# Top-k attention and an exact-GELU MLP: the order of searches, reciprocals and larger halves on DVE, and two more items in 36 by squares

## The chip, the cores and the metric

The kernel runs on one NeuronCore of a Trainium2 chip. The metric is the device time of one execution in microseconds. The core's engines run their own instruction streams and wait for each other by semaphores: TensorE (PE), VectorE (DVE), ScalarE (ACT), GpSimd (POOL), and SyncE (SP), which here issues nearly all DMAs.

## The reference

Attention over 8 batches, 8 heads, 576 rows, head size 64, that keeps the 32 largest scores of each row, and behind it an MLP of 4608 tokens, 512 to 2048 to 512, with exact GELU; all in float32:

```python
scores = scale * np.matmul(q, k.transpose(0, 1, 3, 2))
kth = np.partition(scores, -top_k, axis=-1)[..., -top_k:-top_k + 1]
scores = np.where(scores >= kth, scores, -1e9)
attn = np.exp(scores - max); attn = attn / (sum(attn) + 1e-09)
x = (attn @ v) -> (tokens, heads * 64)
out = gelu(x @ w_in) @ w_out
```

## The kernel before

**Items.** An item is 128 query rows of a pair of heads: a tile of 128 partitions by 2 x 576 scores. There are 18 items for each batch, N = 144 in all. A ring is 36 items (`RINGS = 36`), two batches; places in it repeat, so "item 5 of 36" stands for items 5, 41, 77 and 113.

**Slots.** The whole program is written out by a Python loop over n (L1205), one slot for each item, and the order in which it emits instructions is the order of each engine's stream. Slot n works on several items at once:

- PE makes the scores of items n + 2 (and n + 3); ACT copies them out of PSUM (`scores`, L396).
- DVE makes the larger of each score and its partner 288 columns on (`larger`, L442, row L446). POOL makes the smaller ones from an integer sum (`sum_up` L472, `smaller` L481). The first two searches then need only half the columns. Items 18 to 27 of the first ring (`SINGLE`) go without and are searched over all 576.
- DVE finds the 32 largest of item n in four rounds (`top_k`, L487): MAX8 gives eight largest, MATCH_REPLACE8 strikes them out, for each of the two heads. The first round writes the tile `first`, whose first value is the row maximum. The second pair of rounds searches all 576.
- `threshold` (L522): two small POOL instructions make the bias terms from the 32nd largest value and the maximum (L527, L528).
- `select` and `softmax` (L542, L552): ACT pushes what is below the threshold far down (Prelu, L547), and makes the exponentials with their sum (L559). These are for item n - 1 in slot n. `add_small` (L536, row L540, POOL) adds 1e-9 to the sum, `inverse` (L530, row L534, DVE) takes the reciprocal, `normalise` (L566, row L582, POOL) multiplies.
- Item n - 2 is turned over, so that keys lie on partitions. In one way PE transposes it (one transposition of the ends, L666, eight of the rest, L680) and ACT copies the result out of PSUM into the tile `pt` (L669, L695). In the other way, "by squares", DVE transposes squares of 32 x 32 in place (`square_p`, L610, row L614, in the middle of `top_k(n)`), SP writes the tile to DRAM in four DMAs (`write_p`, L616, row L624) and reads it back one slot later in another order (`read_p`, L626, row L634) into `pt`. From item 27 on, even items go by squares (but for 12 of 36), and of the odd ones those in `LATER` (L594), in the rings after the first and up to item 135 (`moved`, L596).
- The product with v (`attend`, L729, row L751) is made for a pair of items, even and odd, which share the single `pt` tile, in slot n of odd item n - 3, right behind the scores. Where the odd item is one of `LATER`, it is made one slot later, between pieces of the MLP.
- Between all this PE works off pieces of the MLP in a fixed number for each slot (`room_in`, L1141; `bare`, L1137, gives two pieces to a slot whose product has moved away and takes them from the slot before): first layer (L820), gelu on ACT (L836), second layer (L976, L938, L941, and `seven`, L974, which ACT copies out by L995).

**What sets the order around the change.** DVE's stream at the end of slot n, by `last()` (L1346): last search of item n, larger halves of n + 2 where `few[0]` holds (slots from 13 on), reciprocal of n - 1. Then come, in slot n + 1, the squares of new q and k tiles (L294 to L298), where there are any, and the first search of n + 1. On POOL stand in slot n, in this order, `smaller(n + 1)`, `add_small(n - 1)`, `threshold(n)`, `normalise(n - 1)`, `sum_up(n + 2)`, then sums of the MLP. `lists` (halves) and `first` have two buffers each, `pt` has one, the score tiles `s` seven.

Of the kernel before, what the change touches and what calls it, by code (L numbers as in the profile page):

```python
# [14 lines left out]
def kernel(  # L15
# [19 lines left out]
    nc = tc.nc  # L35
    f32, i32, u32 = mybir.dt.float32, mybir.dt.int32, mybir.dt.uint32
# [5 lines left out]
    P = 128  # L42
# [20 lines left out]
    work = ctx.enter_context(tc.tile_pool(name="work", bufs=2))  # L63
# [46 lines left out]
    def flush():  # L110
        held[0] = False
        while late_issues:
            late_issues.pop(0)()
        late_issues.extend(later)
        later.clear()
# [142 lines left out]
    for b in range(B):  # L258
# [4 lines left out]
        last = [(b * NP + p, NM) for p in range(0, NP, 2)]  # L263
# [8 lines left out]
    N = len(items)  # L272
# [4 lines left out]
    few = [False]  # L277
# [55 lines left out]
    S_of, stat_of = {}, {}  # L333
# [95 lines left out]
    lists_of = {}  # L429
    HS = S // 2  # L430

    def paired(i):

        return PAIRED <= i < N and i not in SINGLE

    def halves_of(i):
        s = S_of[i].rearrange("p (e h n) -> p e h n", e=2, h=2)
        return s[:, :, 0], s[:, :, 1]
# [3 lines left out]
    def larger(i):  # L442

        if paired(i) and i not in have_larger:
            have_larger.add(i)
            nc.vector.tensor_tensor(lists_for(i)[:, :, 0], *halves_of(i), op=ALU.max)  # L446

    def into_of(i):

        if i < 2 and i not in into_lists:  # L450
            into_lists[i] = work.tile([P, 2, 2, HS], f32, tag="pt", bufs=1, name="into")
        return into_lists.get(i, lists_of[i])
# [13 lines left out]
    def lists_for(i):  # L466

        if i not in lists_of:
            lists_of[i] = work.tile([P, 2, 2, HS], f32, tag="lists", name="lists")
        return lists_of[i]  # L470
# [10 lines left out]
    def smaller(i):  # L481

        if paired(i):
            both, top = lists_of[i][:, :, 1].bitcast(i32), lists_of[i][:, :, 0].bitcast(i32)
            nc.gpsimd.tensor_tensor(into_of(i)[:, :, 1].bitcast(i32), both, top, op=ALU.subtract)  # L485

    def top_k(i, last, middle):  # L487


        stat_of[i] = st = {  # L490
            "first": work.tile([P, 2, 8], f32, tag="first", name="first"),
        }
        stat = work.tile([P, 4, 2], f32, tag="stat", name="stat")
        st.update((n, stat[:, x]) for x, n in enumerate(("neg", "bias", "den", "rden")))
        top = work.tile([P, 2, 16], f32, tag="top", bufs=1, name="top")
        into = [st["first"]] + [
            top[:, :, 8:16] if r == TOPK // 8 - 1 else top[:, :, 0:8] for r in range(1, TOPK // 8)
        ]
        if paired(i):
            t = lists_of[i]  # L500
            u = into_of(i)
            both = u.rearrange("p e h n -> p e (h n)")
            rounds = [(t[:, :, 0], u[:, :, 0]), (u[:, :, 0], u[:, :, 0])]
            rounds = [(*(rounds[r] if 16 * r < TOPK else (both, both)), x) for r, x in enumerate(into)]
        else:
            s = S_of[i].rearrange("p (e n) -> p e n", e=2)
            t = work.tile([P, 2, S], f32, tag="lists", name="rest")
            rounds = [(s if r == 0 else t, t, x) for r, x in enumerate(into)]
        for r, (src, dst, x) in enumerate(rounds):
            if 16 * r == TOPK:  # L510
                middle()
            for e in range(2):
                nc.vector.max(x[:, e], src[:, e])  # L513
            if r < len(rounds) - 1:
                for e in range(2):
                    nc.vector.match_replace(dst[:, e], x[:, e], src[:, e], LOWEST)  # L516
            if r == len(rounds) - 1:
                last()

        st["kth"] = top[:, :, 15]  # L520

    def threshold(i):  # L522

        if i < 0 or i >= N:
            return
        st = stat_of[i]
        nc.gpsimd.tensor_scalar(st["neg"], st["kth"], -1.0, None, op0=ALU.mult)  # L527
        nc.gpsimd.tensor_tensor(st["bias"], st["kth"], st["first"][:, :, 0], op=ALU.subtract)  # L528

    def inverse(i):  # L530
        if i < 0 or i >= N:
            return
        st = stat_of[i]
        nc.vector.reciprocal(st["rden"], st["den"])  # L534

    def add_small(i):  # L536
        if i < 0 or i >= N:
            return
        st = stat_of[i]
        nc.gpsimd.tensor_scalar(st["den"], st["den"], 1e-9, None, op0=ALU.add)  # L540
# [50 lines left out]
            return i % RINGS != RINGS // 2 - 1  # L591
        return moved(i) or (i % 2 == 0 and i % RINGS != 12)

    LATER = (3, 13, 25, 31)  # L594

    def moved(i):  # L596

        return RINGS <= i < N - 8 and i % RINGS in LATER

# [7 lines left out]
    RINGS = 2 * len(items) // B  # L607
    turned = {}

    def square_p(i):  # L610

        if squared(i):
            s = S_of[i]
            nc.vector.transpose(s, s)  # L614

    def write_p(i):  # L616

        if squared(i):
            turned[i] = d = dram.tile([SQ, NJ + NM, P // SQ, P], f32, tag="turned", name="turned")
            s = S_of.pop(i).rearrange("p (x j) -> p x j", j=SQ)  # L620
            d = d.rearrange("i c k n -> i (c k) n")
            for a in range(P // SQ):
                rows = slice(a * SQ, (a + 1) * SQ)
                nc.sync.dma_start(out=d[:, :, rows], in_=s[rows])  # L624
# [498 lines left out]
    def mlp(n):  # L1123
        for _ in range(n):
            if done[0] >= len(pieces) or pieces[done[0]][0] > ready[0] or left[0] == 0:
                return
            pieces[done[0]][1]()
            done[0] += 1
            left[0] -= 1
            if eager[0]:  # L1130
                run_gelus()
                run_small(9)
# [58 lines left out]
    first = {2: (0, 1, 1), 3: (2, 2, 3)}  # L1191
    prep_in, squares_in = {}, {}
    for pair in range(2, n_pairs):
        b, p = divmod(pair, NP)
# [10 lines left out]
    for n in range(ahead):  # L1205
# [87 lines left out]
        if few[0]:  # L1293
            room = ODD if n % 2 else 0
            if mid and (mid[0] in starts_next or mid[0] % RINGS == LATER[0]):
                mlp(1)
# [34 lines left out]
            softmax(n - 1, 1)  # L1331
        if n > 0:
            smaller(n + 1)
        add_small(n - 1)
        for piece in tr[-1:] + prep:
            piece(None)
            mlp(1)
# [6 lines left out]
        run_gelus()  # L1344
        if n < N:
            def last():  # L1346
                if few[0]:
                    larger(n + 2)
                inverse(n - 1)

            top_k(n, last, lambda: square_p(n - 2))
            write_p(n - 2)
            flush()
            if n == 0:
                larger(1)
        else:
            inverse(n - 1)
        threshold(n)
        if n == 0:
            smaller(1)  # L1360
        normalise(n - 1)
# [59 lines left out]
```

## Time and profile before

| | |
|---|---|
| median of 3 runs | 1461.84 us (1461.5 to 1461.9) |
| the profiled execution | 1461.3 us |
| its span, first to last instruction | 1459.5 us |
| granted TensorE clock | 1.0 |
| DVE: searches L513 over 576 columns, lists | 528 of 739 ns |
| DVE: larger halves L446 | 133 of 799 ns |
| DVE: squares L614 | 68 of 1365 ns |
| POOL: normalise L582 | 135 of 2109 ns |

The profile gives for each engine the time in which it was busy; a row of the timeline gives start, length, engine, line, operation, tiles (written <- read) and, in brackets, an idle time ahead of it with what ended it. A row with "x8" merges eight instructions of one kind; its length goes from the first's start to the last's end. Matmuls overlap: the time from one start to the next is less than the length of one. A row of grouped instructions ends in busy time, mean length in ns, and the engine's idle time ahead of them. A row of stretches has the stretch, its length, then busy time and count for PE, weight loads, DVE, ACT and POOL.

### The profile page before, as it was taken

The numbers are of one execution on the slowest core, as the hardware profiler recorded it, in microseconds if no ns is written. First come the engines' busy times: TensorE is split into PE (matmuls) and PEld (weight loads), VectorE is DVE, ScalarE is ACT, GpSimd is POOL, SyncE is SP. The second block draws the span as 40 slices with busy tenths as digits, with TensorE's granted clock in tenths as the row PEclk, the third lists the DMA queues.
The fourth block names the chain that finished last, engine by engine and source line by source line (L and its number), as shares of the span: only waits on it lengthen the run. The fifth ranks groups of instructions, "written<-read, shape, count | busy, mean of one in ns | idle before, by whom it ended". The sixth has DMA issues, their size and how long they took to land.

```text
span 1459.5 us, 26550 instructions
## 1 busy us (share of the span) xinstructions
PE 1442.6 (99%) x8621; PEld 1123.9 (77%) x8621; DVE 1329.6 (91%) x3339; ACT 1056.4 (72%) x1883; POOL 1128.4 (77%) x1290
## 2 busy tenths in 40 slices
PE   8999999999999999999999999999999999999999
PEld 6776678877777777787777778787777777787887
DVE  7999999999999999999999999999999999999601
ACT  7999977777777777767777777777676767677620
POOL 6877657877798878878888878887788887878632
PEclk9999999999999999999999999999999999999999
DMA  7524310045454446456554365456554444543200
GB/s 196 150 87 126 84 48 1 9 98 104 90 113 89 87 87 142 82 113 128 111 99 96 65 117 116 90 112 127 117 102 106 90 80 84 127 98 85 53 15 15
DMA packets 591819, 136.49 MB, mean 94 GB/s; under 512 B 504352, under 2 KB 583232, under 8 KB 591680
## 3 DMA queue, kind: packets, MB, share of 16 engines
q1 hardware_dynamic: 590416, 134.37, 43.5%
q8 instruction: 68, 1.11, 0.3%
q14 instruction: 71, 0.58, 0.1%
q10 hardware_dynamic: 1200, 0.39, 0.1%
q0 software_dynamic: 64, 0.03, 0.0%
HBM read 85.19 MB, written 49.55 MB: 92 GB/s over the span
## 4 chain that ended last, share of the span: by engine, by line
PE 44%; POOL 11%; DVE 7%; issue 3%; ACT 3%; DMA 1%; SPq 0%; DVEq 0%; POOLq 0%; ACTq 0%
PE h_ps L820 17%; PE y_ps L976 11%; PE o L751 5%; PE s_ps L408 3%; POOL s L582 3%; DVE top L513 3%; DVE lists L516 2%; POOL lists L485 2%; POOL lists L477 2%; PE seven L974 2%; PE tp L680 2%; PE y_ps L938 2%; PE y_ps L941 1%; DMA turned<-s 1%; DVE s L614 1%
## 5 line engine op out<-in xcount | busy, mean ns | idle before, releaser
L820 PE MATMUL h_ps<-xT,w_in_sb 128*128 128x256 f32 (+1 forms) x2560 | 533.0, 361 | 0.0
L820 PEld LDWEIGHTS h_ps<-xT,w_in_sb 128*128 128x128 f32 x2560 | 438.9, 191 | 69.2 <-issue 10.9
L513 DVE MAX8 top<-lists 128x8 f32<-128x576 f32 (+1 forms) x792 | 475.9, 641 | 0.0
L547 ACT ACTIVATE s<-s,stat 128x576 f32<-128x576 f32 x288 | 219.2, 786 | 123.0 <-POOL stat L527 122.9
L516 DVE MATCH_REPLACE8 lists<-top,lists 128x288 f32<-128x288 f32 (+1 forms) x528 | 308.0, 589 | 0.0
L582 POOL TENSOR_TENSOR s<-s,stat 128x1152 f32<-128x1152 f32 x135 | 284.8, 2109 | 10.1 <-DVE stat L534 5.3
L559 ACT ACTIVATE s<-s,stat 128x576 f32<-128x576 f32 x288 | 225.2, 787 | 7.6
L485 POOL TENSOR_TENSOR lists<-lists 128x576 int32<-128x576 int32 x132 | 186.6, 1413 | 3.1
L477 POOL TENSOR_TENSOR lists<-s 128x576 int32<-128x576 int32 x133 | 188.2, 1415 | 0.0
L540 POOL TENSOR_SCALAR stat<-stat 128x2 f32<-128x2 f32 x144 | 44.4, 309 | 163.0 <-ACT s L559 156.1
L751 PE MATMUL o<-pt,raw_v 128*64 128x256 f32 x1280 | 152.9, 384 | 1.0 <-ACT pt L685 0.4
L416 ACT ACTIVATE s<-s_ps 128x1024 f32<-128x1024 f32 x127 | 126.4, 1046 | 35.2 <-PE s_ps L408 35.0
L751 PEld LDWEIGHTS o<-pt,raw_v 128*64 128x64 f32 x1280 | 86.8, 136 | 80.9 <-issue 38.1
L976 PE MATMUL y_ps<-w_out_sb,sum 128*128 128x256 f32 x472 | 140.4, 379 | 0.0
L408 PE MATMUL s_ps<-kt,qm 64*128 64x512 f32 x512 | 131.2, 621 | 1.1 <-ACT s L414 0.8
L836 ACT ACTIVATE g<-h_ps 128x512 f32<-128x512 f32 x144 | 78.2, 595 | 66.6 <-PE h_ps L820 66.0
L446 DVE TENSOR_TENSOR lists<-s 128x576 f32<-128x576 f32 x133 | 106.2, 799 | 17.8 <-ACT s L381 5.8
L976 PE MATMUL y_ps<-w_out_sb,g 128*128 128x256 f32 x480 | 116.4, 382 | 0.0
L516 DVE MATCH_REPLACE8 lists<-first,lists 128x288 f32<-128x288 f32 x264 | 114.4, 439 | 0.0
L513 DVE MAX8 first<-lists 128x8 f32<-128x288 f32 x268 | 105.8, 434 | 0.0
L976 PEld LDWEIGHTS y_ps<-w_out_sb,g 128*128 128x128 f32 x480 | 90.4, 190 | 15.0 <-issue 3.1
L976 PEld LDWEIGHTS y_ps<-w_out_sb,sum 128*128 128x128 f32 x472 | 89.8, 190 | 12.1
(162 smaller groups left out, 2359.0 us busy)
## 6 DMA issues: line engine op xcount, KB each, us to landing
turned<-s SPq DMA_DIRECT2D x272, 144.0 KB, 3.6
pt<-turned SPq DMA_DIRECT2D x272, 144.0 KB, 3.2
raw_v<-in_v_dram SPq DMA_DIRECT2D x64, 128.0 KB, 2.5
raw_q<-in_q_dram SPq DMA_DIRECT2D x112, 72.0 KB, 2.3
raw_k<-in_k_dram SPq DMA_DIRECT2D x112, 72.0 KB, 2.4
out_dram<-y SPq DMA_DIRECT2D x30, 256.0 KB, 3.1
w_out_sb<-in_moe_w_in_dram SPq DMA_DIRECT2D x14, 511.8 KB, 4.9
w_out_sb<-in_moe_w_out_dram SPq DMA_DIRECT2D x10, 511.8 KB, 4.1
```

The source lines that it names most:

```text
L408: nc.tensor.matmul(s_ps[:, e], lhsT=q_t[rows, :], rhs=kt[rows, main_keys(pair)], start=True, stop=True)
L416: nc.scalar.activation(spread(s, S + TL, SM), s_ps, func=AF.Copy, scale=scale)
L477: nc.gpsimd.tensor_tensor(t[:, :, 1].bitcast(i32), a.bitcast(i32), b.bitcast(i32), op=ALU.add)
L485: nc.gpsimd.tensor_tensor(into_of(i)[:, :, 1].bitcast(i32), both, top, op=ALU.subtract)
L513: nc.vector.max(x[:, e], src[:, e])
L516: nc.vector.match_replace(dst[:, e], x[:, e], src[:, e], LOWEST)
L547: nc.scalar.activation(s, s, func=AF.Prelu, bias=st["neg"][:, e : e + 1], scale=1.0, alpha=STEEP)
L559: nc.scalar.activation(s, s, func=AF.Exp, bias=st["bias"][:, e : e + 1], scale=1.0, accum_out=st["den"][:, e : e + 1],)
L582: nc.gpsimd.tensor_tensor(s, s, wide, op=ALU.mult)
L751: nc.tensor.matmul(o[e * D : (e + 1) * D, 0:n], lhsT=vt[:, j, e, :], rhs=pt[:, e * NJ + j if j < NM else NM, :], start=(j == 0), stop=(j = ...
L820: nc.tensor.matmul(h_tile(u)[:, i, :], lhsT=w_in_sb[:, ko, f * P : (f + 1) * P], rhs=xT[:, ko, c0 : c0 + n], start=(ko == 0), stop=(ko == ...
L976: nc.tensor.matmul(acc[names][:, k], lhsT=lhsT, rhs=rhs, start=(j == 0 and k == 0), stop=(j == FT // 2 - 1 and k == 1),)
```

## The change

- `top_k(i)` no longer makes the first search of its own item always: `first_max(i)` makes it once and remembers it, and `top_k` takes what is there.
- `last()`, behind the last search of item n, now makes the first search of n + 1 ahead of all else (slots 13 on). The larger halves of n + 2 follow there only in slots 15, 17, 19 and 23 of 36 in the rings after the first (`LATE`), and in slot 34 of every ring; in the other slots they are left to the beginning of slot n + 1, where `larger(n + 1)` stood already for what had not been made, and so come behind the reciprocal and ahead of the squares of q and k.
- In the slots of `LATE`, POOL gets `threshold(n)` ahead of `add_small(n - 1)`.
- `LATER` gains 5 and 23: items 41, 77, 113 and 59, 95, 131 go by squares, and their products a slot later.

```diff
-        stat_of[i] = st = {
-            "first": work.tile([P, 2, 8], f32, tag="first", name="first"),
-        }
+        stat_of[i] = st = {"first": first_max(i)}
...
-            for e in range(2):
+            for e in range(2 if r else 0):
                 nc.vector.max(x[:, e], src[:, e])
...
-            if r == len(rounds) - 1:
-                last()
-
         st["kth"] = top[:, :, 15]
+        last()
+
+    first_of = {}
+
+    def first_max(i):
+
+        if i not in first_of:
+            first_of[i] = x = work.tile([P, 2, 8], f32, tag="first", name="first")
+            src = lists_of[i][:, :, 0] if paired(i) else S_of[i].rearrange("p (e n) -> p e n", e=2)
+            for e in range(2):
+                nc.vector.max(x[:, e], src[:, e])
+        return first_of[i]
...
-    LATER = (3, 13, 25, 31)
+    LATE = (15, 17, 19, 23)
+    LATER = (3, 5, 13, 23, 25, 31)
...
-        add_small(n - 1)
+        late_exps = RINGS < n < N - 1 and n % RINGS in LATE
+        if not late_exps:
+            add_small(n - 1)
...
             def last():
-                if few[0]:
+                if few[0] and n + 1 < N:
+                    first_max(n + 1)
+                if late_exps or few[0] and n % RINGS == RINGS - 2:
                     larger(n + 2)
+                if late_exps:
+                    threshold(n)
+                    add_small(n - 1)
                 inverse(n - 1)
...
-        threshold(n)
+        if not late_exps:
+            threshold(n)
```

## The prediction, made before the result was known

> **What bounds the kernel now.** I read the first part of the page, then the busy time by stretches, then the timeline of one ring (the 36 items 72 to 107, from 695.8 to 1037.8 us). Fences of the timeline give rows in order of time, with other engines' rows left out. A slot n is the stretch from DVE's first search of item n to that of item n + 1.
>
> ```profile
> PE 1442.6 (99%) x8621; PEld 1123.9 (77%) x8621; DVE 1329.6 (91%) x3339; ACT 1056.4 (72%) x1883; POOL 1128.4 (77%) x1290
> 695.80:1037.80 342.00, 341.01 (x2014) 266.06 (x2012) 332.98 (x839) 249.08 (x450) 283.51 (x323) 1.00 0.52 105
> 906.12 5.35 PE L820 MATMUL h_ps<-xT,w_in_sb 128*128 128x256 f32 x24
> ```
>
> In the ring PE is busy 341.0 of 342.0 us and DVE 333.0 (the first and third numbers behind the comma in the second row). Busy time of matmuls proves little, since they overlap. What proves it is their spacing: 24 matmuls in 5.35 us, the last one taking 0.38, are 0.216 us from start to start, and the same spacing holds in nearly every group of the ring. So PE streams without a hole. DVE has 9 us of idle time per ring. PE is the bound, DVE is second by 9 us.
>
> The holes that PE does have, in slot 25 (item 97's) and, first, slot 23:
>
> ```profile
> 915.83 1.39 PE L762 MATMUL o<-pt,raw_v 128*64 128x64 f32 x40 [0.26 <-ACT p L995]
> ...
> 932.93 0.76 DVE L446 TENSOR_TENSOR lists<-s 128x576 f32<-128x576 f32 x1
> 933.02 0.75 POOL L540 TENSOR_SCALAR stat<-stat 128x2 f32<-128x2 f32 x1
> 933.85 0.22 POOL L527 TENSOR_SCALAR stat<-top 128x2 f32<-128x2 f32 x1
> 934.10 1.44 ACT L547 ACTIVATE s<-s,stat 128x576 f32<-128x576 f32 x2 [3.62 <-POOL stat L527]
> 937.35 0.59 PE L976 MATMUL y_ps<-w_out_sb,sum 128*128 128x256 f32 x2
> 937.83 0.38 ACT L995 COPY p<-seven 128x256 f32<-128x256 f32 x1
> 938.26 0.49 PE L373 MATMUL tp_t<-kt,qm 128*128 128x128 f32 x2 [0.32 <-ACT p L995]
> ```
>
> This is the chain that ties PE to DVE in odd slots: last search of the item (DVE), threshold (POOL L527), selection (ACT L547, two halves), gelu (L836, not shown), copy of `seven` (L995), which frees the PSUM bank for the keys matmul (PE L373). Two matmuls of L976 take 0.43 us of PE, so L373 was due at 937.78 and came 0.48 late. The room that the same chain has in slot 11, two slots behind the place where item 5 will now be multiplied:
>
> ```profile
> 802.79 0.38 ACT L995 COPY p<-seven 128x256 f32<-128x256 f32 x1
> 803.43 0.39 PE L373 MATMUL tp_t<-kt,qm 128*128 128x128 f32 x2
> ```
>
> From 803.17 to 803.43: 0.26 us. The two engines run in step, with little between them.
>
> **Part one: items 5 and 23 by squares** (41, 77, 113, 59, 95, 131: six items; 131 is still below 136). PE loses the transposes of L666 and L680 and keeps the keys matmul.
>
> ```profile
> 785.82 1.04 PE L680 MATMUL tp<-ident,s 128*128 128x128 f32 x8
> 786.70 0.60 PE L976 MATMUL y_ps<-w_sum,g 128*128 128x256 f32 x2
> 787.13 0.59 PE L976 MATMUL y_ps<-w_out_sb,sum 128*128 128x256 f32 x2
> 787.66 1.99 PE L408 MATMUL s_ps<-kt,qm 64*128 64x512 f32 x8
> ```
>
> From start to start the eight take 0.88 us, 0.11 each; with the one of L666 it is 0.99 per item, 5.9 for six. Against it: the item's product with v (L751, 20 matmuls) leaves its place behind the scores and goes a slot later between two MLP pieces, as item 97's does now:
>
> ```profile
> 971.00 0.60 PE L941 MATMUL y_ps<-w_out_sb,g 128*128 128x256 f32 x2
> 971.53 2.38 PE L751 MATMUL o<-pt,raw_v 128*64 128x256 f32 x20
> 973.84 0.70 PE L938 MATMUL y_ps<-w_out_sb,g 128*128 128x256 f32 x2
> 974.37 0.60 PE L941 MATMUL y_ps<-w_out_sb,g 128*128 128x256 f32 x2
> ```
>
> A pair of pieces takes 0.43; here 0.53 before the group and 0.53 behind it. Behind scores these two tenths are paid by the scores anyway (787.13 to 787.66 is 0.53 too). So 0.2 us per item comes back, 1.2 for six. PE saves 4.7 net. ACT loses the copies out of PSUM (L669, L695) and gains nothing; the number of MLP pieces is unchanged, two go from slots 7 and 25 to 8 and 26.
>
> DVE gains one transpose per item:
>
> ```profile
> L614 DVE STREAM_TRANSPOSE s<-s x68: 1355/1366/1373, 298.7 to 1362.5; 128x1152 f32<-128x1152 f32 x68
> turned<-s SPq DMA_DIRECT2D x272, 144.0 KB, 3.6
> ```
>
> 1.37 us each, 2.7 per ring: 333.0 + 2.7 = 335.7, against PE's 342.0 - 1.6 = 340.4. DVE stays second by over 4 us, so I cost it at nothing in the sum. If the cover were gone it would cost 8.2. SP gets four writes and four reads more per item, 48 over the run. A write lands after 3.6, a read likewise, and from the square in slot i + 2 to the product in slot i + 4 there are more than one and a half slots, some 15 us (342.0 / 36 = 9.5 a slot). What stands behind them in that queue are loads of q, k and v, which are early. I take nothing.
>
> **Part two: the order on DVE.** Now, behind an item's last search, come larger halves of n + 2 (L446), reciprocal of n - 1 (L534), and only then the next item's first search.
>
> ```profile
> 749.73 1.40 DVE L513 MAX8 top<-lists 128x8 f32<-128x576 f32 x2
> 751.24 0.78 DVE L446 TENSOR_TENSOR lists<-s 128x576 f32<-128x576 f32 x1
> 751.39 0.67 POOL L528 TENSOR_TENSOR stat<-top,first 128x2 f32<-128x2 f32 x1
> 751.93 0.15 DVE L534 RECIPROCAL stat<-stat 128x2 f32<-128x2 f32 x1
> 752.01 0.79 DVE L513 MAX8 first<-lists 128x8 f32<-128x288 f32 x2
> 752.16 2.11 POOL L582 TENSOR_TENSOR s<-s,stat 128x1152 f32<-128x1152 f32 x1
> ...
> 924.17 0.17 DVE L534 RECIPROCAL stat<-stat 128x2 f32<-128x2 f32 x1 [1.01 <-POOL stat L540]
> ```
>
> L446 starts 0.11 us after the search ends, because it overwrites the list just searched. The first search of n + 1 needs nothing of that and fills the hole: 0.11 x 36 = 4 us of DVE per ring. In slot 23 the reciprocal waits 1.01 us for the sum of exponentials (L540); with 0.79 of search and 0.78 of larger halves ahead of it most of that goes too, and I take the like for 15, 17 and 19, the other late slots. DVE gains up to 8 us per ring from both; none is in the sum, since PE is the bound. It pays for the squares. In the late slots POOL also does the threshold of n before the sum of n - 1, for which it had to wait: selection of n may start sooner by that wait, and ACT, which does n - 1 until then, has no use for it. Nothing.
>
> What does count is POOL. L528 took 0.67 beside L446, and L540 took 0.75 in slot 25's chain, where L527, no smaller, takes 0.22 without L446. With a search in L446's place the threshold of an odd slot's chain comes some 0.5 earlier. That is the 0.48 hole of slot 25: 1.4 us over three rings. The hole of slot 23 starts at ACT, behind PE's own work, and stays. In return L446 now stands where POOL wants to normalise: DVE's next instruction follows the reciprocal 0.08 after its start, POOL's L582 0.23 after, so L446 is first and L582 is held about 0.6.
>
> ```profile
> 742.75 2.10 POOL L582 TENSOR_TENSOR s<-s,stat 128x1152 f32<-128x1152 f32 x1
> 745.70 1.35 DVE L614 STREAM_TRANSPOSE s<-s 128x1152 f32<-128x1152 f32 x1
> ...
> L513 DVE MAX8 first<-s 128x8 f32<-128x576 f32 x20 | 14.0, 740 | 0.0
> 226.91 2.11 POOL L582 TENSOR_TENSOR s<-s,stat 128x1152 f32<-128x1152 f32 x1
> 230.52 0.27 PE L666 MATMUL tp_t<-ident,s 128*128 128x128 f32 x1
> ```
>
> The squares have 0.85 us behind L582 (slot 5), 0.2 after that: still hidden. In items 18 to 27 of the first ring, the next search is of 576 columns (740 ns, twice) and puts the reciprocal up to 1.5 later; the transposes there have 1.5 us in the tightest place I found (226.91 + 2.11 to 230.52): hidden, barely.
>
> The row behind this: two DVE inputs and POOL exclude each other.
>
> ```profile
> 721.88 1.39 POOL L485 TENSOR_TENSOR lists<-lists 128x576 int32<-128x576 int32 x1
> 722.83 1.07 DVE L446 TENSOR_TENSOR lists<-s 128x576 f32<-128x576 f32 x1
> ```
>
> L446 lasted 1.07 instead of 0.78 and ended 0.63 after L485 did. The Trainium skill ("SBUF — State Buffer", section "SBUF: two separate sides") says that a DVE instruction with two SBUF inputs and a GpSimd one lock the shared port pair for a whole instruction, and that the other fully blocks; the trace agrees. That rule speaks against the change wherever L582 gets there first; it is the third rival.
>
> **Sum.** The profiled execution took 1461.3 us, 0.5 below the median of 1461.8. 1461.3 - 5.9 + 1.2 - 1.4 = 1455.2; on the median's scale 1455.7, and I say 1455.6.
>
> **The rivals.**
> 1. PE stalls anew and the gain is eaten: no change. A square delays all that follows it on DVE by 1.37, and PE comes 0.8 earlier: 2.2 together, against 0.26 in slot 11. DVE's gains must make up for it, and should: 0.5 by POOL, 0.11 a slot, the waits of slots 15 to 23. If half of the 2.2 is missing, each of the six items stalls PE by about 1: 1455.7 + 6 = 1461.5.
> 2. Slower, at the same place: if the searches bring DVE forward by nothing, PE waits 2.2 - 0.3 = 1.9 for each of the six, 11.4 against the 4.7 saved: 1468.5. The sign turns where a moved item costs over 0.8 of new stall. For it speaks the 0.26, against it that the hole ahead of L446 is one of order, which the change takes away.
> 3. L446 loses the race to L582 and waits out its 2.11, about 2 us of DVE for each loss. Two losses a ring use up DVE's 4 us; in all 31 slots of a ring that have the new order it would be some 55 us a ring, over 1600 in all. Against it: 0.08 before 0.23.
> 4. DVE is the bound after all, and PE's spacing only follows. Then the 9 us of idle time go, less 2.7: 6 us a ring, 1443. The Trainium skill ("Perfetto Trace Analysis", section "Identifying the Most-Contended Engine") judges PE by its weight loads, 77% here, which makes DVE with 91% the busiest; the even spacing says otherwise.
>
> **Chances.** About 0.2% (2.9 us) is what a measurement of this kernel can tell from no change. Forecast 0.70, with 1453.5 to 1458.5 as its own range: below, the 1.2 of switching is not paid and the hole of slot 23 closes too (0.26 idle, three times, 0.8: 1455.6 - 2.0 = 1453.6); above, the 1.4 is not won and the first ring's later reciprocals cost one 1.5 (1458.5). Rival 1 has 0.14, rival 2 0.10, rival 3 0.04, rival 4 0.02. Faster: forecast, 4 and a part of 1 (0.04): 0.76; same 0.10; slower 0.14. The range goes from 1453 to 1461.3 and leaves out 2 to 4.
>
> **What would show it.** Six more of L614, six fewer of L666, 48 fewer of L680; no 0.11 before L446, and L446 right behind L534 in most slots; L528 near 0.2; L582 starting up to 0.6 later; hardly a wait of L534 for L540; PE's spacing unchanged, no stall in front of L373 in slot 25. Stalls of PE ahead of L373 in slots 9, 11 and 27, or an L446 of 2 us, would make me wrong.

## The result and the profile after

| kernel | us, median (lowest to highest) | runs |
|---|---|---|
| before | 1461.59 (1461.21 to 1462.77) | 21 |
| changed | 1458.55 (1458.28 to 1461.52) | 21 |

The ratio is 0.9980, with a 95% interval of 0.9974 to 0.9987: faster by 3.0 us, a little under half of the 6.2 forecast. The profiled execution of the changed kernel is the slowest of its runs, so rows of single moments below come from the same kernel run again (1458.4 us, span 1456.5 us), and only the counts and means from its own page. That page, its first part and four groups (the columns are busy us and mean ns of one, then idle time of the engine before them and what ended it):

```profile
PE 1439.8 (99%) x8567; PEld 1121.3 (77%) x8567; DVE 1324.4 (91%) x3345; ACT 1050.2 (72%) x1871; POOL 1131.3 (78%) x1290
...
L589 POOL TENSOR_TENSOR s<-s,stat 128x1152 f32<-128x1152 f32 x135 | 311.2, 2305 | 30.9 <-DVE stat L541 29.9
...
L547 POOL TENSOR_SCALAR stat<-stat 128x2 f32<-128x2 f32 x144 | 31.3, 217 | 136.1 <-ACT s L566 129.3
...
L446 DVE TENSOR_TENSOR lists<-s 128x576 f32<-128x576 f32 x133 | 103.9, 781 | 2.1 <-ACT s L381 2.0
...
L622 DVE STREAM_TRANSPOSE s<-s 128x1152 f32<-128x1152 f32 x74 | 100.8, 1363 | 0.0
```

From L522 on the new line numbers are 7 or 8 higher: the square L614 is L622, the reciprocal L534 is L541, the sum L540 is L547, the normalising L582 is L589, the selection L547 is L554, the transposes L680 are L688. PE has 54 matmuls fewer and DVE six squares more, as the change says.

The new stall is in slot 9 of each later ring. Rows of ACT and PE from the timeline of the changed kernel run again, slot 9 of the third ring:

```profile
777.94 1.44 ACT L554 ACTIVATE s<-s,stat 128x576 f32<-128x576 f32 x2 [6.01 <-POOL stat L534]
779.40 1.28 ACT L844 ACT_TABLE_LOAD   x1
780.69 1.09 ACT L844 ACTIVATE g<-h_ps 128x512 f32<-128x512 f32 x2
781.66 0.38 ACT L1003 COPY p<-seven 128x256 f32<-128x256 f32 x1
782.06 1.28 ACT L566 ACT_TABLE_LOAD   x1
782.96 0.59 PE L984 MATMUL y_ps<-w_out_sb,sum 128*128 128x256 f32 x2
783.35 0.78 ACT L566 ACTIVATE s<-s,stat 128x576 f32<-128x576 f32 x1
784.13 0.35 ACT L764 COPY xT<-o 128x256 f32<-128x256 f32 x1
784.53 1.09 PE L688 MATMUL tp<-ident,s 128*128 128x128 f32 x8 [0.97 <-ACT xT L764]
```

The product of item 5 and the eight transposes of item 7 use the same PSUM tile in turn (`pair_tile` serves `o` and `tp`, and some of the scores). PE must wait until ACT has copied the product out (L764), and on ACT that copy stands behind the selection of item 8 (L554), two table loads, a gelu, the copy of `seven` and an exponential. ACT itself idled 6.01 us ahead of that selection, because the threshold (POOL L534) was late, and the threshold follows DVE's last search. Two matmuls of L984 take 0.43, so the transposes were due at 783.39 and came 1.14 late.

### The profile page after: what moved, and what is told of

Same layout as the page of the kernel before. It is cut to its first block, busy times and chain, and to the rows that moved or that the text cites. A ratio compares the mean times of both kernels' runs of the same rounds, so it can differ in the third digit from the quotient of the medians.

```text
span 1459.6 us, 26560 instructions
## 1 busy us (share of the span) xinstructions
PE 1439.8 (99%) x8567; PEld 1121.3 (77%) x8567; DVE 1324.4 (91%) x3345; ACT 1050.2 (72%) x1871; POOL 1131.3 (78%) x1290
## 5 line engine op out<-in xcount | busy, mean ns | idle before, releaser
L589 POOL TENSOR_TENSOR s<-s,stat 128x1152 f32<-128x1152 f32 x135 | 311.2, 2305 | 30.9 <-DVE stat L541 29.9
L554 ACT ACTIVATE s<-s,stat 128x576 f32<-128x576 f32 x288 | 217.7, 778 | 127.1 <-POOL stat L534 126.9
L759 PE MATMUL o<-pt,raw_v 128*64 128x256 f32 x1280 | 153.0, 384 | 1.9 <-DMA pt<-turned 1.3
L759 PEld LDWEIGHTS o<-pt,raw_v 128*64 128x64 f32 x1280 | 87.3, 137 | 78.9 <-issue 34.4
L984 PE MATMUL y_ps<-w_out_sb,sum 128*128 128x256 f32 x472 | 140.5, 379 | 0.0
L547 POOL TENSOR_SCALAR stat<-stat 128x2 f32<-128x2 f32 x144 | 31.3, 217 | 136.1 <-ACT s L566 129.3
L408 PE MATMUL s_ps<-kt,qm 64*128 64x512 f32 x512 | 129.9, 620 | 0.8 <-ACT s L414 0.8
L984 PE MATMUL y_ps<-w_out_sb,g 128*128 128x256 f32 x480 | 118.0, 383 | 0.0
L446 DVE TENSOR_TENSOR lists<-s 128x576 f32<-128x576 f32 x133 | 103.9, 781 | 2.1 <-ACT s L381 2.0
L984 PEld LDWEIGHTS y_ps<-w_out_sb,g 128*128 128x128 f32 x480 | 90.0, 190 | 16.9 <-issue 5.4
L622 DVE STREAM_TRANSPOSE s<-s 128x1152 f32<-128x1152 f32 x74 | 100.8, 1363 | 0.0
```

Source lines behind the costliest of these rows:

```text
L408: nc.tensor.matmul(s_ps[:, e], lhsT=q_t[rows, :], rhs=kt[rows, main_keys(pair)], start=True, stop=True)
L554: nc.scalar.activation(s, s, func=AF.Prelu, bias=st["neg"][:, e : e + 1], scale=1.0, alpha=STEEP)
L589: nc.gpsimd.tensor_tensor(s, s, wide, op=ALU.mult)
L759: nc.tensor.matmul(o[e * D : (e + 1) * D, 0:n], lhsT=vt[:, j, e, :], rhs=pt[:, e * NJ + j if j < NM else NM, :], start=(j == 0), stop=(j = ...
L984: nc.tensor.matmul(acc[names][:, k], lhsT=lhsT, rhs=rhs, start=(j == 0 and k == 0), stop=(j == FT // 2 - 1 and k == 1),)
```

## The experiments

All kernels compute everything, but for the one without DVE's transposing of items 5 and 23, which leaves that step out. The table has the medians; the ratio is to runs of the kernel before on the same chip.

| run | us | ratio, 95% interval |
|---|---|---|
| changed kernel again | 1458.91 | 0.9983 [0.9974, 0.9991] |
| order alone | 1457.89 | 0.9972 [0.9962, 0.9983] |
| items alone | 1468.31 | 1.0042 [1.0030, 1.0055] |
| without DVE's transposing of 5 and 23 | 1455.51 | 0.9957 [0.9944, 0.9969] |
| without item 5 | 1456.89 | 0.9966 [0.9953, 0.9978] |
| early copy of 5 | 1456.82 | 0.9965 [0.9951, 0.9979] |
| early copies of 5 and 31 | 1457.19 | 0.9967 [0.9955, 0.9979] |
| early copies of 5, 23 and 31 | 1456.56 | 0.9965 [0.9952, 0.9977] |
| order alone, early copy of 31 | 1456.95 | 0.9966 [0.9953, 0.9978] |
| items 9 and 21 instead | 1464.27 | 1.0022 [1.0013, 1.0031] |
| the same with early copies | 1459.91 | 0.9989 [0.9980, 0.9998] |
| item 5 with early copies, 23 as before | 1456.09 | 0.9963 [0.9950, 0.9977] |

Where the time lies is read from stretches of PE: from the start of the product (L751, L759 after) of one item to that of another, in us.

| kernel | item 37 to 47 | 57 to 73 | 93 to 109 | 129 to 139 |
|---|---|---|---|---|
| before | 92.70 | 151.98 | 152.39 | 94.12 |
| order alone | 92.34 | 151.61 | 151.61 | 93.53 |
| changed, again | 92.90 | 151.21 | 151.15 | 93.56 |
| without DVE's transposing of 5 and 23 | 91.83 | 151.14 | 151.16 | 92.74 |
| early copy of 5 | 92.12 | 151.19 | 151.20 | 93.37 |
| items alone | 93.99 | 153.03 | 151.76 | 94.93 |

The first column holds what item 5 does (73 to 83 and 109 to 119 differ in the same way within 0.05 us, but for the items alone, +1.29, +1.64 and +1.33 to before), the last what item 23 does, and the two between them that and slots 35 and 4 as well. Each value is from one execution.

### The same kernel again, the copy of item 5 early, item 5 left out, the order alone

The first of these has no edit. The others, each on the changed kernel:

```diff
# early copy of 5
-            if mid and (mid[0] in starts_next or mid[0] % RINGS == LATER[0]):
+            if mid and (mid[0] in starts_next or mid[0] % RINGS in (3, 5)):
# without item 5
-    LATER = (3, 5, 13, 23, 25, 31)
+    LATER = (3, 13, 23, 25, 31)
# order alone
-    LATER = (3, 5, 13, 23, 25, 31)
+    LATER = (3, 13, 25, 31)
```

> The changed kernel unaltered, profiled once more. The first profile of it shows two things that may belong to that one execution: 2.2 us more by item 6, and 1.34 us of PE waiting for a read of squares in slot 24 of one ring (item 93's product). All theories: about 1458.5, with the 1.14 us hole ahead of the eight transposes (L688) in slot 9 of all three later rings, and, if the two things are of the execution, neither of them.

> Item 5's product, and with it ACT's copy of it to xT, is put ahead of the first exponential in slot 9, as is done for item 3. Theory A (the hole of slot 9 is the PSUM tile: item 7's transposes wait until ACT has copied item 5's product out of it, and that copy stands behind a table load and an exponential): the copy comes some 2 us earlier, the holes of 3 x 1.14 go, 1455.1. Theory B (DVE's added square of item 5 makes the threshold late, and all that follows on ACT with it): the chain starts no earlier, the copy still gains those 2 us, so the time falls too, but L534 is where it was; B is told from A by leaving the square out. Theory C (the six items save less on PE than reckoned): no change, 1458.5.

> Item 5 goes by PE again, 23 stays by squares. A and B: the three holes of 1.14 go (3.4) and the net saving of three items (0.79 each, 2.4) is given up: 1457.5. C with a saving near nothing: 1455.1.

> The order on DVE and POOL alone, neither item added. If the prediction's first part was right, this gains what it put down to the earlier threshold, the 0.48 us hole of slot 25 in three rings, and the late product of one ring: 1461.6 - 1.4 - 0.5 = 1459.7. A rival (DVE is the bound): over 3 us a ring, below 1452.

The order alone gains 3.9 us (1461.75 to 1457.89), more than the whole change, and both squares together lose 0.7 to 1.0 of it (1458.55 and 1458.91). Item 5 is the loser: 92.90 against 92.34 in its stretch, 0.55 a ring, and 1456.89 for the kernel without it (1457.5 expected). With its product and copy ahead of the first exponential it is 92.12, a small gain in place of a loss, and the stall in slot 9 is gone; the time is 1456.82, where 1455.1 was expected. So the wait for the copy is the stall; but it isn't all of the missing gain, since 92.12 is 0.22 under the order alone and not the 0.79 reckoned. Matmul by matmul, the early copy takes 1.20 us away in slot 9 and brings 0.45 back in slot 10, where the scores now wait for the copy of the late transposes:

```profile
788.14 1.13 PE L408 MATMUL s_ps<-kt,qm 64*128 64x512 f32 x4 [0.18 <-ACT pt L703]
```

What the order alone takes away and makes, by the groups of PE of both kernels (idle time of PE is behind the second bar). Before:

```profile
L680 PE MATMUL tp<-ident,s 128*128 128x128 f32 x536 | 69.6, 273 | 0.0
L373 PE MATMUL tp_t<-kt,qm 128*128 128x128 f32 x104 | 20.5, 279 | 1.1 <-ACT p L995 1.0
```

The order alone:

```profile
L688 PE MATMUL tp<-ident,s 128*128 128x128 f32 x536 | 69.7, 273 | 0.6 <-ACT xT L764 0.6
L373 PE MATMUL tp_t<-kt,qm 128*128 128x128 f32 x104 | 20.0, 274 | 0.0
```

And the changed kernel, again:

```profile
L688 PE MATMUL tp<-ident,s 128*128 128x128 f32 x488 | 63.7, 273 | 2.9 <-ACT xT L764 2.9
L373 PE MATMUL tp_t<-kt,qm 128*128 128x128 f32 x92 | 18.0, 277 | 0.0
```

The stall of slot 25 ahead of the keys (L373) goes, as forecast. The rest of the order's 3.9 us are holes that the prediction did not list. In slots 4 and 12 scores (L408) waited 0.2 to 0.3 us for the copies out of the transposes' PSUM tile (L695), followed by another 0.1 each time; in the order alone these are not there. The scores of slot 4 of the third ring, before and with the order alone; PE idles in the middle of the first group, which is 0.30 longer:

```profile
732.55 2.29 PE L408 MATMUL s_ps<-kt,qm 64*128 64x512 f32 x8
```

```profile
731.62 1.99 PE L408 MATMUL s_ps<-kt,qm 64*128 64x512 f32 x8
```

Both kernels have the same 8621 matmuls in the same order, so their spacing can be compared one by one. The order wins 0.58 in slot 25 of each ring (1.7 in all), 0.3 to 0.4 in slots 4 and 12 each (2.0 in all) and 0.4 once ahead of a product in slot 35; it loses 0.53 in slot 35 of two rings (1.1), where the transposes wait for item 31's copy (0.47 late, then 0.05 more). That makes 3.0 of the 3.3 us between the two profiled executions.

### The items alone, DVE's transposes left out, and more early copies

```diff
# items alone, on the kernel before
-    LATER = (3, 13, 25, 31)
+    LATER = (3, 5, 13, 23, 25, 31)
# without DVE's transposing of 5 and 23, on the changed kernel
-            nc.vector.transpose(s, s)
+            if not (moved(i) and i % RINGS in (5, 23)):
+                nc.vector.transpose(s, s)
# early copies of 5 and 31, on the changed kernel
-            if mid and (mid[0] in starts_next or mid[0] % RINGS == LATER[0]):
+            if mid and (mid[0] in starts_next or mid[0] % RINGS in (3, 5, 31)):
# order alone, early copy of 31: LATER = (3, 13, 25, 31), and
+            if mid and (mid[0] in starts_next or mid[0] % RINGS in (3, 31)):
```

> The kernel before with only part one of the change: items 5 and 23 of each later ring take their squares on VectorE, and VectorE's order stays as it was. The prediction's sum for this part was 4.7 us less (1456.9). Theory A (the copy of xT stands behind ScalarE's queue while the next transposes wait for the PSUM tile that the product holds): item 5 loses about 0.54 us per ring, as between the change and the order alone, and item 23 brings nothing by itself, so 1461.7 + 1.6 = about 1463 us, with a stall of about 1 us ahead of the eight transposes in slot 9 of each ring. Theory C (only the saving on TensorE is smaller than reckoned, no stall): about 1460 us and no such stall.

> The changed kernel with VectorE's transposing of the squares of items 5 and 23 left out (part of the computation is left out, so the product of these items has wrong weights; the copies, products and waits stay). Theory B (what VectorE was given, 2.7 us per ring, delays its chain, and with it the threshold and the exponential ahead of which ScalarE's copy stands): the stall of 1.1 us in slot 9 shrinks and the time goes towards the predicted 1455.6 us. Theory A (the copy's place in ScalarE's queue makes the stall, and VectorE has room): within 0.5 us of the changed kernel, 1458.0 to 1459.0 us, with the stall of 1.1 us still there.

> The changed kernel with the product and the copy of items 5 and 31 put ahead of the first exponential on ScalarE, as those of item 3 already are. Theory A: the stall of slot 9 goes as in the run with item 5 alone (1456.8 us), and what is left at slot 35, 0.1 to 0.5 us in a ring, goes with it: 1455.5 to 1456.7 us. If the place in slot 35 is not what sets the end there: 1456.8 us.

> VectorE's new order alone (items 5 and 23 by transposes on TensorE, 1457.9 us) with the product and copy of item 31 put ahead of the first exponential. Theory A: the 0.47 us ahead of the keys' transposes in slot 35 of the rings 1 and 2 goes, 2 x 0.5 = 1.0 us less: about 1456.9 us. If something else holds these transposes: 1457.9 us.

These two settle most of it, and theory A as I had put it falls. The items alone make the kernel 6.2 us slower; I had expected 1.6 at most. The parts do not add up: -3.9 and +6.2 would be +2.3, and the change is -3.0. Without DVE's transposing the time is 1455.51: six transposes on DVE, 8.2 us of work, cost 3.0 to 3.4 us of the time, though PE, ACT and the queues do the same in both kernels. So the square delays the chain, as theory B says, and the copy's place is only where PE meets it. That 1455.5 is also what was forecast for the whole change is chance: it has 2.5 us more from the order than the forecast, and stalls that the forecast had not.

The lateness can be read off. The selection of item 8 (L547, L554 after) against the product of item 1 (L751, L759 after), five slots ahead, in timelines of the third ring. Before:

```profile
734.78 0.44 PE L751 MATMUL o<-pt,raw_v 128*64 128x256 f32 x2
...
779.67 1.44 ACT L547 ACTIVATE s<-s,stat 128x576 f32<-128x576 f32 x2 [2.34 <-POOL stat L527]
```

The order alone:

```profile
733.53 0.44 PE L759 MATMUL o<-pt,raw_v 128*64 128x256 f32 x2
...
777.37 1.44 ACT L554 ACTIVATE s<-s,stat 128x576 f32<-128x576 f32 x2 [1.31 <-POOL stat L534]
```

The changed kernel, again (its selection stands in the fence of slot 9):

```profile
733.05 0.65 PE L759 MATMUL o<-pt,raw_v 128*64 128x256 f32 x4
```

Without DVE's transposing, where the added line makes L688 to L689:

```profile
732.53 0.44 PE L760 MATMUL o<-pt,raw_v 128*64 128x256 f32 x2
...
776.36 1.44 ACT L554 ACTIVATE s<-s,stat 128x576 f32<-128x576 f32 x2 [4.90 <-POOL stat L534]
...
782.55 0.35 ACT L765 COPY xT<-o 128x256 f32<-128x256 f32 x1
782.96 1.09 PE L689 MATMUL tp<-ident,s 128*128 128x128 f32 x8
```

The items alone:

```profile
737.17 0.44 PE L751 MATMUL o<-pt,raw_v 128*64 128x256 f32 x2
...
783.18 1.44 ACT L547 ACTIVATE s<-s,stat 128x576 f32<-128x576 f32 x2 [6.23 <-POOL stat L527]
...
787.34 0.49 PE L373 MATMUL tp_t<-kt,qm 128*128 128x128 f32 x2 [0.60 <-ACT p L995]
...
789.78 0.44 PE L680 MATMUL tp<-ident,s 128*128 128x128 f32 x2 [0.98 <-ACT xT L756]
```

The distances are 44.89 before, 43.84 with the order alone, 44.89 in the changed kernel, 43.83 without the transposing and 46.01 with the items alone. The order brings the selection forward by 1.05; item 5's square, two slots earlier, takes all of it back; without the new order it comes 1.12 later than before, and PE stalls twice in slot 9, ahead of the keys and of the transposes. PE, which has lost about 0.8 us of work there, comes earlier in all kernels that move item 5. Without DVE's transposing PE's eight transposes come 0.2 late, not 1.14.

With the same matmuls in the same order, PE's spacing can be compared one by one between the changed kernel and the one without the transposing. The changed kernel loses 1.05 us in slot 9 of every ring and 0.8 to 0.9 over slots 27 to 29, there in four small pieces (ahead of keys, scores, an MLP piece and the transposes of item 27, 0.05 to 0.25 each with another 0.05 to 0.1 behind it). Slot 27 of the third ring, the changed kernel again:

```profile
954.11 0.59 PE L984 MATMUL y_ps<-w_out_sb,sum 128*128 128x256 f32 x2
954.29 0.38 ACT L1003 COPY p<-seven 128x256 f32<-128x256 f32 x1
954.72 0.49 PE L373 MATMUL t_ps<-kt,qm 128*128 128x128 f32 x2
```

Two matmuls of L984 take 0.43, so the keys were due at 954.54; they start at 954.72, behind the end of L1003's copy, and the two take 0.49 in place of 0.38. Against this stand 0.86 us in slot 35 of two rings, where the kernel without the transposing waits for item 31's copy and the changed one does not (more on slot 35 below).

Why DVE cannot take the square there shows in its busy time over slots 4 to 10 (the third number behind the comma; the first two are PE and PEld). Before, the order alone, and the changed kernel again:

```profile
733.12:799.72 66.60, 66.56 (x355) 51.01 (x352) 65.41 (x165) 46.96 (x84) 59.71 (x70) 1.00 0.49 98
```

```profile
730.71:795.04 64.33, 64.33 (x345) 48.94 (x344) 63.89 (x164) 47.51 (x87) 57.34 (x66) 1.00 0.49 98
```

```profile
730.21:795.61 65.40, 64.43 (x338) 48.25 (x337) 65.17 (x164) 46.35 (x85) 57.80 (x67) 1.00 0.57 114
```

In seven slots DVE idles 1.2 us before, 0.4 with the order alone and 0.2 in the changed kernel. It takes 64.33 for them with the order alone, 65.40 with item 5's square, and 64.33 again without the transposing: the square makes the seven slots 1.07 longer. The 9 us of idle time per ring lie elsewhere.

Early copies of 5 and 31 bring no more than that of 5 (1457.19 and 1456.82, intervals one upon the other): a miss for theory A, and the changed kernel has no stall in slot 35 of those rings, so there was nothing to win (151.21 and 151.15 us in the table, 151.22 and 151.23 with both copies early). Where slot 35 does stall, in the order alone, item 31's early copy takes off 0.9 us, as expected.

Why slot 35 stalls in some kernels and not in others stands two slots ahead of it. Slot 33 of the third ring, the order alone and the changed kernel again:

```profile
1005.07 2.11 POOL L589 TENSOR_TENSOR s<-s,stat 128x1152 f32<-128x1152 f32 x1
1005.59 2.20 DVE L446 TENSOR_TENSOR lists<-s 128x576 f32<-128x576 f32 x1 [0.72 <-ACT s L381]
```

```profile
1005.73 0.78 DVE L446 TENSOR_TENSOR lists<-s 128x576 f32<-128x576 f32 x1
1005.86 2.62 POOL L589 TENSOR_TENSOR s<-s,stat 128x1152 f32<-128x1152 f32 x1
```

In the order alone DVE waits for ACT's copy of the scores (L381), POOL's normalising starts first, and the larger halves take 2.20 in place of 0.78, until 0.61 after POOL is done. In the second and third ring of all fourteen traces, slot 35 stalls only where L446 took 2.2 us or more in slot 33: in both rings of the order alone, of the kernel without the transposing and of items 9 and 21, and in one ring of the changed kernel's first profile. Where it took that long and slot 35 did not stall, item 31's copy was early.

### Other items, and what is left of the copies

If DVE's idle time decides, items whose squares fall beside it should pay. The order alone idles 1.3 us in slot 11 and 1.4 in slot 24.

```diff
# items 9 and 21, on the changed kernel
-    LATER = (3, 5, 13, 23, 25, 31)
+    LATER = (3, 9, 13, 21, 25, 31)
# the same with early copies, also
+            if mid and (mid[0] in starts_next or mid[0] % RINGS in (3, 9, 21, 31)):
# early copies of 5, 23 and 31, on the changed kernel
+            if mid and (mid[0] in starts_next or mid[0] % RINGS in (3, 5, 23, 31)):
```

> The changed kernel with items 9 and 21 in place of 5 and 23, nothing else. Their squares stand in slots 11 and 23, where VectorE, by the windows of the order alone, still idles 1.2 us in slot 11 and 1.35 us in slot 24, while it has no idle time in the slots 4 to 10 and 26 to 31 where those of 5 and 23 stand. Theory B (a square costs what VectorE has no idle time for before the next exponential that ScalarE's copy waits for): most of the 0.79 us for each item comes through, 1457.9 - 4.7 = 1453.2, at most 1455 us. Theory A (the copy's place in ScalarE's queue alone): stalls of 0.5 to 1.1 us per item stay, 1457 to 1459 us.

> As the run with items 9 and 21, with the products and copies of items 9, 21 and 31 put ahead of the first exponential too, as that of item 3 is. If the copies still make stalls there (theory A): up to 1 us less than the run with items 9 and 21 in each ring; if they do not (theory B), only the 0.5 us of slot 35 in two rings, about 1 us less at most, so 1452.3 to 1455 us.

> The changed kernel with the copies of items 5, 23 and 31 all ahead of the first exponential. Theory A: the 0.35 us of slot 27 goes too, 1.0 us less than the run with items 5 and 31 (1457.2), about 1456.2 us. Theory B: VectorE stays 1.2 us late in the slots 27 to 32 and the wait moves to the next copy or threshold, 1456.8 to 1457.5 us.

A plain miss: 1464.27 where 1453.2 was expected, worse than items 5 and 23. Slots 11 and 13 of the third ring with items 9 and 21:

```profile
798.79 0.17 DVE L541 RECIPROCAL stat<-stat 128x2 f32<-128x2 f32 x1 [1.30 <-POOL stat L547]
...
802.71 1.37 DVE L622 STREAM_TRANSPOSE s<-s 128x1152 f32<-128x1152 f32 x1
...
822.63 0.49 PE L373 MATMUL tp_t<-kt,qm 128*128 128x128 f32 x2 [0.61 <-ACT y L1000]
...
825.07 1.10 PE L688 MATMUL tp<-ident,s 128*128 128x128 f32 x8 [0.97 <-ACT xT L764]
```

DVE's idle time in slot 11 is a wait of the reciprocal for the sum of ACT's exponentials (L547), at the beginning of the slot. The square stands behind it, in the middle of the searches. It cannot be done during the wait, so the wait stays 1.30 and the next searches come 1.27 us later than with the order alone. That idle time is a part of the same loop (search, threshold, exponential, sum, reciprocal), not room in it. With item 21 it is otherwise: the wait of 1.4 us in slot 24 stands behind its square (slot 23), and in this run it is gone in all three rings. The searches, set against the order alone from slot 11 on, are 1.3 late at the start of slot 23, 2.6 at that of slot 24 and 1.1 at that of slot 25. So the wait here takes up work that is put ahead of it, and none that is put behind it. PE's transposes wait for item 21's copy even so (0.85 us idle in slot 25 of the third ring). Early copies take the stalls ahead of L688 away and 4.4 us with them, of which 1.1 is item 31's in slot 35; the one ahead of L373 stays. The early copy of item 23 gains little (1456.56 to 1457.19): the 0.2 us ahead of the keys in slot 27 is not a wait for its own copy and stays, and 0.29 that goes ahead of the scores there comes back in slot 28, as theory B says.

### The version that came out best

```diff
# on the changed kernel
-    LATER = (3, 5, 13, 23, 25, 31)
+    LATER = (3, 5, 13, 25, 31)
-            if mid and (mid[0] in starts_next or mid[0] % RINGS == LATER[0]):
+            if mid and (mid[0] in starts_next or mid[0] % RINGS in (3, 5, 31)):
```

> VectorE's new order, item 5 by squares with its copy and that of item 31 ahead of the first exponential, item 23 by transposes on TensorE as before. By the stretches of the runs so far, each to the kernel before: the products of items 1 to 11 take 0.55 us less in each of three rings (the runs with an early copy of item 5), items 21 to 37 take 0.9 and 1.3 us less in two rings and 0.6 in the last (the run of the order with item 31's copy early): 1461.7 - 1.65 - 2.8 = 1457.2, less what the start brings (the order alone was 0.8 better than its stretches add up to): 1456.4 us. If items 5 and 23 help each other: 1456.8 us or more.

1456.09 us (1456.4 expected): 5.6 us under the kernel before and 2.5 under the changed one. Its transposes wait for no copy:

```profile
L688 PE MATMUL tp<-ident,s 128*128 128x128 f32 x512 | 66.5, 273 | 0.0
```

Six kernels lie between 1456.1 and 1457.2 with intervals that overlap, so which of them is best is not settled. That this one beats the changed kernel is: its slowest run (1457.26) lies under the fastest of the changed kernel's 21 (1458.28), though the intervals of the two ratios touch.

## Why the prediction was wrong

It said 1455.6; it was 1458.55. The direction was right. That the time lies inside the wide range (1453 to 1461.3) is luck: two errors of opposite sign made it up. It lies just outside the 1453.5 to 1458.5 that the forecast's own mechanism was given.

**The step that failed** is, in part one, "DVE stays second by over 4 us, so I cost it at nothing in the sum". It weighed the squares against DVE's idle time of a whole ring. In the slots where these squares stand there is next to none (with the order alone 0.4 us in slots 4 to 10, 0.1 in slots 26 to 31), so the square makes later thresholds late: item 5's puts the selection in slot 9 back by 1.05 of its 1.37 us. Left out, the squares free 1.05 us of PE in slot 9 and 0.8 to 0.9 in slots 27 to 29, 5.7 us over three rings, less 1.7 in slot 35. Of the 4.0 that this makes, 3.0 to 3.4 show in the times; the profiled execution without the transposing is 0.6 late from its first ring on, which is the rest.

**The account.** PE's saving of 0.79 per item (0.99 less 0.2) was right: without DVE's transposing the last column falls from 93.53 to 92.74, just that. Against the order alone, item 5 then lost 0.55 where it should have won 0.79, so 1.34 of stall a ring (0.3 of it stays even without the transposing), and item 23 lost 0.03 in the last ring where it should have won 0.79, so 0.82. From the time before: 1461.6 - 3.9 (the order) - 4.7 (PE's saving) + 4.0 + 2.5 (these stalls, three rings) - 0.95 (the stall of slot 35 that the order alone has twice) = 1458.55, the measured time. It closes because the stalls are themselves differences between these kernels; what it shows is where the time went. The forecast had -1.4, -4.7 and no stall.

**The place of the stall** was missed with it. The moved product was priced by item 97's at 0.2 us of switching. That its PSUM tile is the one that the next transposes need, and that ACT's copy stands behind the exponential, was not looked at; the rows of item 97 show no stall. "Stalls of PE ahead of L373 in slots 9, 11 and 27" was the wrong line to watch in slot 9: it is L688. In slot 27 the keys do wait, so that sign held.

**Part two** was priced at 1.4 us, the hole of slot 25, and brought 3.9 by itself. The hole did go. The waits of L408 in slots 4 and 12, 0.65 us a ring, were not looked for, since I called the spacing even and listed the two holes that I had found. Without this second error, which is 2.5 us the other way, the first would have shown in full.

**Rivals 1 and 2** had the mechanism: a square delays DVE's chain by 1.37, PE comes 0.8 earlier, together 2.2. With the new order 1.05 of it is made up, close to the half for which rival 1 gave a stall of about 1 for each item. That is what came (1.34 and 0.82); rival 1's total of 1461.5 (its own terms, 1455.7 and 6, make 1461.7) did not, because the order brought more. Rival 2, searches that bring DVE forward by nothing, is the run of the items alone, 1468.31 where it had 1468.5. Rival 4 did not happen as a whole: taking 8.2 us off DVE brought 3.0 to 3.4, so DVE sets the time in some stretches (slots 4 to 10 among them) and not in all.

**The reciprocal** was to lose its waits for the sum. What ended DVE's idle time ahead of it, us and times, before and in the changed kernel's first profile:

```profile
  POOL stat L540: 27.8, 27
```

```profile
  POOL stat L547: 51.8, 54
```

They nearly doubled: much of what DVE gains by the earlier search, it waits for at the reciprocal. "Up to 8 us per ring" to pay squares with was therefore not there; at the selection of item 8 the gain was 1.05.

**POOL.** The sum (L540 before) had a mean of 309 ns and has 217 as L547: without L446 beside them POOL's small instructions are short, as foreseen. L582 was to be held about 0.6; as L589 it does not wait for L446, but lasts longer where L446 is under way. The changed kernel again, slot 9:

```profile
786.44 0.73 DVE L446 TENSOR_TENSOR lists<-s 128x576 f32<-128x576 f32 x1
786.60 2.54 POOL L589 TENSOR_TENSOR s<-s,stat 128x1152 f32<-128x1152 f32 x1 [0.41 <-DVE stat L541]
```

2.54 against 2.10 elsewhere: 0.44 more, with 0.57 of overlap; on the page its mean rose to 2305 ns. The Trainium skill ("SBUF — State Buffer", section "SBUF: two separate sides") has GpSimd blocked while a DVE instruction with two SBUF inputs holds the shared port pair; the trace agrees, and the delay shows in the duration. Rival 3, L446 losing the race, came true in a few places: three of the 133 in the changed kernel's first profile took 2.2 to 2.4 us, all in slot 33, which is the sign that the prediction gave for being wrong. It is far from the two losses in each ring that the rival needed, and the mean of L446 stays at 781 ns; but the stalls of slot 35 stand only behind such rows, though no run changes that alone.

Left open: what decides, between kernels that differ only in slots 5 to 27, whether ACT's copy in slot 33 comes in time for L446; and why the first ring and its start take up to 2.4 us longer in some executions (item 37's product starts between 391.6 and 394.0 us in the kernels with the new order).

## What to carry to other kernels

Work moved to the second-busiest engine is free only if that engine idles between the place of the work and the next instruction that somebody waits for; read its idle time slot by slot, and see what ended it, since a wait inside the loop is no room for work that stands behind it in the engine's stream. For a moved step, list the buffers that it shares with its new neighbours and who frees them, and what stands in that engine's queue ahead of the freeing. Two parts of a change that work on the same chain don't add up (-3.9 and +6.2 gave -3.0), so each is worth its own run.

## What had not been expected of the hardware

- A wait costs PE more than the idle time beside its row: in slot 9 the row has 0.97 us, and the transposes start 1.14 after their due time, since PE's matmuls overlap and the row counts from the end of the last one.
- ACT's table loads, 1.28 us each, twice between the selection and the copy in slot 9, are two fifths of that chain (777.94 to 784.48), though ACT is idle for 28% of the span. From the end of the selection (779.38) to the start of the gelu (780.69) a switch takes 1.31. The Trainium skill ("ScalarE: Activation LUTs", section "What ACT_TABLE_LOAD costs") gives 1.28 for the load, which the trace shares, and 1.38 for a drain beside it, which does not show here.
